# The even half of a real transform folded a second time: matmuls of 256 columns in place of 512, in a kernel whose order is planned

## The chip, the cores and the metric

The kernel runs on one core of a Trainium2 chip. A core has five engines that run side by side: PE (TensorE, matrix products into PSUM, with a weight load before each), DVE (VectorE), ACT (ScalarE), POOL (GpSimd) and SP (SyncE, which here only issues DMAs). The metric is the device time of one execution in microseconds (us).

## The reference

The input is one sequence `x` of 2048 rows (S) and 1024 columns (D), in bf16. Two branches are mixed by a gate:

```python
g = sigmoid((x * gate_w).sum(-1, keepdims=True))
a = irfft2(rfft2(x) * (w_r + 1j * w_i), s=(S, D))        # branch A: a 2-D spectral filter
Lam_bar = exp(dt * Lam);  B_bar = ((Lam_bar - 1) / Lam)[:, None] * Bmat
h[t] = Lam_bar * h[t - 1] + B_bar @ x[t]                 # branch B: a linear recurrence with 1024 complex states
b = 2 * (h @ Cmat.T).real + x * Dskip
out = g * a + (1 - g) * b
```

## The kernel before

**Branch B.** The states are cut into eight blocks `jb` of 128 and the sequence into four chunks `c` of 512. A turn `(jb, pr)` covers two chunks. `bu` computes `B x` for it on PE (L809: 16 matmuls of 512 columns for each chunk, real and imaginary), ACT copies the result from PSUM to a tile `u` (L812), and DVE turns it by a table of sines and cosines (`rot`, L777 to L783, through the scratch tile `su`, of which there is one), runs the recurrence as a real scan (L821) and passes the end state on as a carry. `rot_out` turns the states back. `table(jb)` makes the tables: nine ACT operations and three DVE operations for each block. There are three `u` tiles, so PE can run at most three turns ahead of DVE. At the end `yout(tb)` multiplies, for each of 16 row blocks, all states by C (L853, 32 matmuls of 512 columns), adds the skip term (L860), and DVE mixes in branch A (L880).

**Branch A.** The transform along D comes first. `halves(c)` writes, from the transposed input `xT`, the sums (L421) and differences (L423) of columns d and d + 512 into `xpm`: the sums give the even frequencies k, the differences the odd ones. `fd(j)`, for 16 strips j of 128 rows, multiplies each half by its matrix `G` (L560): four matmuls of 512 columns for each half (256 frequencies, real and imaginary), accumulated over four blocks of 128 columns. The rows of a strip are 16 apart in the sequence, so the weights of these matmuls are read from `xpm` at every 16th element. One ACT copy (L565) moves the strip to SBUF and interleaves even and odd frequencies. `s1(j)` does the first half of the transform along S (L575, L576: four matmuls of 512 columns), copied by ACT (L579; L580 saves one column) and written to DRAM. `s2w` reads back turned, finishes the transform (L700) and multiplies by the filter on DVE (L705); `is1`, `is2` and `idft` are the way back (L716, L735, L751, with ACT copies at L720, L739 and L756). Column 0 needs a repair, `fixup`, which uses `Wc`, two columns of the filter loaded in pieces of 2 bytes.

**The order.** Nothing of this is issued as it is written. Every helper records operations with an engine, a key, an assumed duration and the items it reads and writes. `Plan.run` then walks through time: it takes the engine on which something can start first, and of the operations that can start there (within a slack of 0.05 to 0.1 us on DVE and ACT) the one with the smallest key. The keys come from 28 numbers, `K_T0` to `K_GATE`, which place the stages against each other. So a changed duration or key moves the whole order on every engine, and SP's queue of DMAs with it. PSUM is four slots of two banks, shared by all stages.

Of the kernel before, what the change touches and what calls it, by code (L numbers as in the profile page):

```python
# [14 lines left out]
BF16 = mybir.dt.bfloat16  # L15
# [6 lines left out]
K = 512  # L22
NP = 1024
P = 128
TC = 512
# [10 lines left out]
def _host_consts():  # L36


    d = np.arange(K)[:, None]
    G = np.zeros((K, 2, 2, 256))  # L40
    for par in range(2):
        k = 2 * np.arange(256)[None, :] + par
        ang = 2 * np.pi * (((2 * d + 1) * k) % (2 * D)) / (2 * D)
        G[:, par, 0, :] = np.cos(ang)
        G[:, par, 1, :] = -np.sin(ang)
    G[:, 0, 1, 0] = (-1.0) ** np.arange(K)

    K4 = K // 2
    n = np.arange(K4)[None, :]
    Gi = np.zeros((2, 2, 2, P, K4))  # L50
    for par in range(2):
        for half in range(2):
            k = 2 * (np.arange(P)[:, None] + P * half) + par
            ang = 2 * np.pi * (((2 * n + 1) * k) % (2 * D)) / (2 * D)
            ck = np.where(k == 0, 1.0, 2.0)
            Gi[par, half, 0] = ck * np.cos(ang)
            Gi[par, half, 1] = -2.0 * np.sin(ang)
    Gi[0, 0, 1, 0, :] = (-1.0) ** np.arange(K4)
    Gi /= float(D * S)
    s1 = np.arange(P)[:, None, None, None]  # L60
    s2 = np.arange(16)[None, :, None, None]
    mh = 2 * np.arange(64)[None, None, None, :] + np.arange(2)[None, None, :, None]
    angF = 2 * np.pi * (((16 * s1 + s2) * mh) % S) / S
    TF = np.concatenate([np.sin(angF), np.cos(angF), -np.sin(angF)], axis=3)
    qq = np.arange(64)[:, None, None]
    bb = np.arange(32)[None, :, None]
    uu = np.arange(64).reshape(2, 2, 16).transpose(0, 2, 1).reshape(1, 1, 64)
    angI = 2 * np.pi * (((32 * qq + bb) * uu) % S) / S
    ci, si = np.cos(angI), np.sin(angI)
    MI = np.concatenate([np.concatenate([ci, -si, -ci], axis=2), np.concatenate([si, ci, -si], axis=2)], axis=0)  # L70
    p = np.arange(P)
    q = p // 8
    a = p % 8
    angK = 2 * np.pi * ((q[:, None] * q[None, :]) % 16) / 16
    delta = (a[:, None] == a[None, :]).astype(np.float64)
    Kc, Ks = delta * np.cos(angK), delta * np.sin(angK)
    ang16 = 2 * np.pi * (np.outer(np.arange(16), np.arange(16)) % 16) / 16
    RF = np.zeros((16, 2, 4, 2, 16, 4))
    for i in range(4):
        RF[:, 0, i, 0, :, i], RF[:, 1, i, 0, :, i] = np.cos(ang16), np.sin(ang16)  # L80
        RF[:, 0, i, 1, :, i], RF[:, 1, i, 1, :, i] = np.sin(ang16), -np.cos(ang16)
    ang32 = 2 * np.pi * (np.outer(np.arange(32), np.arange(32)) % 32) / 32
    RI = np.zeros((32, 2, 2, 2, 32, 2))
    for i in range(2):
        RI[:, 0, i, 0, :, i], RI[:, 1, i, 0, :, i] = np.cos(ang32), np.sin(ang32)
        RI[:, 0, i, 1, :, i], RI[:, 1, i, 1, :, i] = np.sin(ang32), -np.cos(ang32)
    sel = np.zeros((2, P, 2, 64))
    for odd in range(2):
        for c in range(2):
            sel[c, 2 * np.arange(64) + odd, odd, np.arange(64)] = 1.0 - 2.0 * c  # L90
    J = np.zeros((P, P))
    J[np.arange(P), 127 - np.arange(P)] = 1.0
    P0 = np.zeros((P, P))
    P0[(128 - np.arange(P)) % 128, np.arange(P)] = 1.0
    bf = lambda z: np.ascontiguousarray(np.ascontiguousarray(z, dtype=np.float32).astype(ml_dtypes.bfloat16))
    return dict(
        G=bf(G.reshape(4, P, 1024).transpose(1, 0, 2)),
        Gi=bf(Gi.reshape(8, P, K4).transpose(1, 0, 2)),
        TF=bf(TF),
        MI=bf(MI),  # L100
        TK=bf(np.stack([Kc, Ks, -Ks, J, P0, RF.reshape(P, P), RI.reshape(P, P)] + [z.reshape(P, P) for z in sel.reshape(2, P, P)], axis=1)),
    )
# [143 lines left out]
def kernel(  # L246
# [17 lines left out]
    nc = tc.nc  # L264
# [26 lines left out]
    def tile_of(shape, dtype, name, tag):  # L291
        group = plan.kinds[tag][0]
        if group == "m":
            return plan.buf(tag, lambda i: view(G_all[:, 1024 * (i - 4):1024 * (i - 3)], shape) if i >= 6 else
                            slots.tile(shape, dtype, name=name, tag=f"{group}{i}"))
        if group == "f":

            return plan.buf(tag, lambda i: view(hbuf[1].t[:, 2 + i // 4, i // 2 % 2, 1024 * (i % 2):1024 * (i % 2 + 1)], shape),
                            host=hbuf[1])
        return plan.buf(tag, lambda i: slots.tile(shape, dtype, name=name, tag=f"{group}{i}"))  # L300
# [11 lines left out]
    def pe(key, us, fn, r=(), w=()):  # L312
        plan.op("PE", key, us + 0.16, fn, r, w, gap=us)
# [4 lines left out]
    def dve(key, us, fn, r=(), w=()):  # L318
        plan.op("DVE", key, us, fn, r, w, gap=us - 0.085)
# [6 lines left out]

    U = 0.216
    A2 = nc.scalar.activation
    K_T0 = -49.82
    K_TB = 24.89  # L330
    K_D = 96.13
    K_O = 186.17
    K_TAB0 = 39.51
    K_TAB = -34.21
    K_F0 = 32.43
    K_F = 0.81
    K_W0 = 55.24
    K_W = 10.37
    K_WI = -61.0
    K_I0 = -398.94  # L340
    K_I = 45.74
    K_ID = 13.66
    K_CT = 34.07
    K_FIX = -104.41
    K_R1 = 397.68
    K_R2 = 838.32
    K_RS = 100.57
    K_Y = 840.08
    K_YS = 125.57
    K_H = 7.06  # L350
    K_XP = -10.85
    K_XS = -46.18
    K_TP = -92.54
    K_DM = 111.49
    K_BT = 77.09
    K_GATE = 165.55
    KX = lambda c: K_XP * (c > 0) + K_XS * max(c - 1, 0)


    vec8 = tile_of([8, 5, P], BF16, "vec8", "tt")  # L360
    for i, src in enumerate((B_Lambda_re, B_Lambda_im, B_log_dt, gate_w, B_Dskip)):
        dma(0, 0.05, lambda i=i, src=src: nc.scalar.dma_start(out=vec8.t[:, i, :], in_=src.rearrange("(j p) -> j p", p=P)),
            w=[(vec8, i)], eng="ACT", issue=0.33)
# [10 lines left out]
    G_sb = G_all.rearrange("p (d r k) -> p d r k", d=4, r=2)  # L374
# [41 lines left out]
    xT_of = lambda c: [("xT", c, q) for q in range(4)]  # L416
    xpm = tile_of([P, 2, 4, S], BF16, "xpm", "b32")

    def halves(c):
        lo, hi = xT[c][:, 0:4, :], xT[c][:, 4:8, :]  # L420
        dve(KX(c) + K_H, 1.22, lambda: nc.vector.tensor_add(out=xpm.t[:, 0, :, TC * c:TC * (c + 1)], in0=lo, in1=hi),  # L421
            r=xT_of(c), w=[(xpm, c, 0)])
        dve(KX(c) + K_H + 0.5, 1.22, lambda: nc.vector.tensor_sub(out=xpm.t[:, 1, :, TC * c:TC * (c + 1)], in0=lo, in1=hi),  # L423
            r=xT_of(c), w=[(xpm, c, 1)])

# [126 lines left out]
    mm = nc.tensor.matmul  # L552

    def fd(j, key):
        pf = psum([P, 2, 2, 256], "ps_fd")

        def f(par):
            xA = xpm.t.rearrange("p h d (a b) -> p h d b a", b=16)
            for db in range(4):
                mm(pf.t[:, par].rearrange("p c k -> p (c k)"), lhsT=xA[:, par, db, j, :],  # L560
                   rhs=G_sb[:, db, par, :], start=(db == 0), stop=(db == 3))
        for par in range(2):
            pe(key, 4 * U, lambda par=par: f(par), r=[(xpm, c, par) for c in range(4)] + [("G",)], w=[(pf, par)])
        X1 = tile_of([P, 2, K], BF16, "X1", "X1")
        act(key, 1.3, lambda: nc.scalar.copy(out=X1.t.rearrange("p c (k r) -> p r c k", r=2), in_=pf.t),  # L565
            r=[(pf, 0), (pf, 1)], w=[(X1,)])
        return X1
# [109 lines left out]
    for i in range(2):  # L677
        dma(30 + 16 * i, 3.0, lambda i=i: nc.sync.dma_start(out=MI_sb[i].t, in_=cst["MI"][:, 16 * i:16 * (i + 1)]),
            r=[("Bcol", 1)] if i else [], w=[(MI_sb[i],)])
# [205 lines left out]

    KB = lambda p, cc: K_T0 + K_TB * (p + 0.5 * cc)
    KD = lambda p: KB(p, 0) + K_D
    KF = lambda j: K_F0 + K_F * j
    KW = lambda b: K_W0 + K_W * b
    KI = lambda bp: K_I0 + K_I * bp  # L890
    halves(0)
# [8 lines left out]
    def turns_of(lo, hi):  # L900
        for p, (jb, pr) in list(enumerate(turns))[lo:hi]:
            if pr == 0:
                tabs[jb] = table(jb, K_TAB0 if jb == 0 else KB(p, 0) - K_TAB)
                if jb:
                    load_BT(jb, KB(max(p - 2, 0), 0) + K_BT)
            carries[jb] = bu(jb, pr, tabs[jb], carries.get(jb), (KB(p, 0), KB(p, 1)), KD(p))
            if pr == 0:
                rot_out(jb, 0, 1, KD(p) + K_O)
                rot_out(jb, 1, 1, K_R1 + K_RS * jb)
            else:  # L910
                rot_out(jb, 2, 2, K_R2 + K_RS * jb)

# [5 lines left out]
    for j in range(16):  # L918
        nxt = fd(j + 1, KF(j + 1)) if j + 1 < 16 else None
        s1(j, X1, KF(j + 1) + 1)  # L920
        X1 = nxt
    fixup(K_FIX)
    dma(130, 2.0, lambda: nc.sync.dma_start(out=G_all[:, 0:4 * K], in_=cst["Gi"].rearrange("p r k -> p (r k)")), r=[("Qz",)], w=[("G",)])
# [4 lines left out]
    for b in range(16):  # L928
        if b + 2 < 16:
            s2w(b + 2, KW(b + 2))  # L930
        is1(b, KW(b) + K_WI)
        if b % 2 and b + 3 < 16:
# [3 lines left out]
    for bp in range(16):  # L936
        nxt = is2(bp + 1, KI(bp + 1)) if bp + 1 < 16 else None
        idft(bp, ZT, KI(bp) + K_ID)
        if bp % 2 == 0:
            load_CT(bp // 2, KI(bp) + K_CT)  # L940
        ZT = nxt
    diag = make_diag(200)
    for tb in range(16):
        yout(tb, K_Y + K_YS * tb, diag)
    with tc.manual_schedule():
# [31 lines left out]
```

## Time and profile before

| what | value |
|---|---|
| median of 3 runs | 340.61 us (339.99 to 342.0) |
| the profiled execution | 340.25 us, span of its instructions 338.5 us |
| PE, matmuls | 327.6 us busy, 1917 instructions |
| PE, weight loads | 171.5 us |
| DVE | 292.0 us, 484 instructions |
| ACT | 192.7 us, 270 instructions |
| POOL | 17.0 us |
| granted TensorE clock | 1.00 |

The span runs from the first instruction to the last of the profiled execution. A matmul's duration in the profile goes on past the start of the next one, so durations of PE add up to more than the time they take; the distance from one start to the next is the step. A row of a group gives busy time, then the mean duration of one in ns, then the engine's idle time just before them and what ended it.

### The profile page before, as it was taken

The page shows a single profiled execution, that of the slowest core. Times are in us where ns is not written, and L with a number is a line of the kernel's source. Part 1 is how long each engine was busy: PE and PEld are TensorE (multiplying, and loading weights), DVE is VectorE, ACT ScalarE, POOL GpSimd, SP SyncE. Part 2 cuts the span into 40 slices and gives each one's busy share as a digit, 9 for nine tenths or more (in the row PEclk, how much of TensorE's full clock was granted, in tenths as well). Part 3 has the DMA queues.
Part 4 walks back from the last instruction along what each step waited for, and adds up shares of the span by engine and source line. Part 5 has one row for each costly group of instructions (what it writes and reads, how often), then busy time and mean ns, then how long its engine had stood idle before and what let it go on. Part 6 is the DMA issues. An engine that isn't in the chain of part 4 may idle for free.

```text
span 338.5 us, 5165 instructions
## 1 busy us (share of the span) xinstructions
PE 327.6 (97%) x1917; PEld 171.5 (51%) x1917; DVE 292.0 (86%) x484; ACT 192.7 (57%) x270; POOL 17.0 (5%) x36
## 2 busy tenths in 40 slices
PE   5999999999999999999998999999999999999994
PEld 4755465655444444444456576544544544445442
DVE  2899999997199999999999999999999999952321
ACT  3796999999887677999689999610000000000000
POOL 1157000000300000000000000000000000000000
PEclk9999999999999999999999999999999999999999
DMA  8995411993668999998487989961131024510001
GB/s 229 385 329 28 64 62 65 253 312 118 198 154 241 263 283 259 300 228 195 124 219 194 305 225 236 247 211 47 45 109 59 7 64 135 200 39 31 31 36 59
DMA packets 68705, 55.76 MB, mean 165 GB/s; under 512 B 46917, under 2 KB 51269, under 8 KB 68553
## 3 DMA queue, kind: packets, MB, share of 16 engines
q1 hardware_dynamic: 68600, 55.43, 60.1%
q8 instruction: 15, 0.25, 0.3%
q14 instruction: 10, 0.07, 0.1%
q10 hardware_dynamic: 80, 0.01, 0.0%
HBM read 30.77 MB, written 16.79 MB: 141 GB/s over the span
## 4 chain that ended last, share of the span: by engine, by line
PE 75%; ACT 13%; DVE 6%; issue 3%; DMA 1%; SPq 0%; DVEq 0%; ACTq 0%
PE ps_y L853 33%; PE psu L809 21%; PE ps_fd L560 7%; PE ps_id L751 3%; PE pt L403 2%; PE ps_y L860 2%; ACT A L579 2%; ACT u L812 1%; PE ps_is L716 1%; PE ps_s L575 1%; PE ps_s L576 1%; PE ps_is L735 1%; PE ps_is L717 1%; ACT ZT L739 1%; DVE h L821 1%
## 5 line engine op out<-in xcount | busy, mean ns | idle before, releaser
L809 PE MATMUL psu<-xT,BTs 128*128 128x512 bf16 x512 | 115.9, 379 | 0.6 <-ACT h L703 0.3
L853 PE MATMUL ps_y<-CT,h 128*128 128x512 bf16 x512 | 113.5, 379 | 0.0
L809 PEld LDWEIGHTS <-BTs 128*128 128x128 bf16 x512 | 49.6, 98 | 59.2 <-issue 1.6
L853 PEld LDWEIGHTS <-h 128*128 128x128 bf16 x512 | 49.2, 98 | 56.7 <-DVE h L779 0.5
L821 DVE TENSOR_TENSOR_SCAN h<-r_sb,carry,u 128x512 bf16<-128x512 f32 x48 | 59.5, 1270 | 0.0
L880 DVE SCALAR_TENSOR_TENSOR o<-ps_y,omg,ga 128x1024 bf16<-128x1024 f32 (+1 forms) x17 | 20.5, 1210 | 25.2 <-PE ps_y L860 25.2
L812 ACT CAST u<-psu 128x1024 bf16<-128x1024 f32 x32 | 32.5, 1019 | 11.0 <-PE psu L809 10.9
L560 PE MATMUL ps_fd<-G_all,xpm 128*128 128x512 bf16 x128 | 30.1, 379 | 0.0
L560 PEld LDWEIGHTS <-xpm 128*128 128x128 bf16 x128 | 18.4, 144 | 9.9
L777 DVE TENSOR_TENSOR su<-u,cs 128x2048 bf16<-128x2048 bf16 x16 | 19.4, 1215 | 2.8 <-ACT u L812 2.7
L565 ACT CAST X<-ps_fd 128x1024 bf16<-128x1024 f32 x16 | 21.3, 1340 | 0.2
L778 DVE TENSOR_TENSOR h<-h,pn 128x1024 bf16<-128x1024 bf16 (+1 forms) x24 | 20.6, 856 | 0.1
L777 DVE TENSOR_TENSOR su<-h,pn 128x1024 bf16<-128x1024 bf16 (+1 forms) x24 | 20.5, 856 | 0.1
L778 DVE TENSOR_TENSOR u<-u,cs 128x2048 bf16<-128x2048 bf16 x16 | 19.5, 1218 | 0.1
L821 DVE TENSOR_TENSOR_SCAN h<-r_sb,u 128x512 bf16<-128x512 f32 x16 | 19.0, 1210 | 0.0
L720 ACT CAST h<-ps_is 128x1024 bf16<-128x1024 f32 x16 | 15.8, 1014 | 2.3 <-PE ps_is L717 2.1
L579 ACT CAST A<-ps_s 128x1024 bf16<-128x1024 f32 x16 | 16.5, 1042 | 0.0
L703 ACT CAST h<-ps_s 128x1024 bf16<-128x1024 f32 x16 | 15.9, 1015 | 0.4 <-PE ps_s L700 0.3
L739 ACT CAST ZT<-ps_is 128x1024 bf16<-128x1024 f32 x13 | 12.9, 1046 | 2.6 <-PE ps_is L735 2.6
L751 PE MATMUL ps_id<-G_all,ZT 128*128 128x256 bf16 x104 | 12.8, 273 | 0.8 <-ACT ZT L739 0.8
L403 PE MATMUL pt<-ident,xn 128*128 128x128 bf16 x128 | 9.7, 243 | 3.7 <-DMA xn<-in_A_x_dram 3.5
L779 DVE TENSOR_TENSOR h<-h,su 128x512 bf16<-128x512 bf16 (+1 forms) x24 | 12.0, 501 | 0.2
(155 smaller groups left out, 388.0 us busy)
## 6 DMA issues: line engine op xcount, KB each, us to landing
xn<-in_A_x_dram SPq DMA_DIRECT2D x16, 256.0 KB, 4.6
turn_scratch<-A SPq DMA_DIRECT2D x16, 256.0 KB, 2.1
h<-turn_scratch SPq DMA_DIRECT2D x16, 256.0 KB, 5.6
turn_scratch<-h SPq DMA_DIRECT2D x16, 256.0 KB, 6.3
out_dram<-o SPq DMA_DIRECT2D x15, 256.0 KB, 2.1
eoc<-ga_scratch SPq DMA_DIRECT2D x12, 256.0 KB, 2.7
Cq<-turn_scratch SPq DMA_DIRECT2D x11, 256.0 KB, 3.6
ga_scratch<-eo SPq DMA_DIRECT2D x11, 256.0 KB, 2.7
```

The source lines that it names most:

```text
L403: nc.tensor.transpose(out=pt.t[:, j8, :], in_=src()[:, P * j8:P * (j8 + 1)], identity=ident)
L560: mm(pf.t[:, par].rearrange("p c k -> p (c k)"), lhsT=xA[:, par, db, j, :], rhs=G_sb[:, db, par, :], start=(db == 0), stop=(db == 3))
L565: act(key, 1.3, lambda: nc.scalar.copy(out=X1.t.rearrange("p c (k r) -> p r c k", r=2), in_=pf.t), r=[(pf, 0), (pf, 1)], w=[(X1,)])
L579: act(key, 1.01, lambda: nc.scalar.copy(out=A1.t, in_=psa.t), r=[(psa,)], w=[(A1,)])
L751: mm(pz.t[:, at, :], lhsT=ZT.t[:, 2 * par + half, c, :], rhs=Gi_sb[:, par, half, c, :], start=(half == 0), stop=(half == 1))
L777: dve(key, w, lambda: nc.vector.tensor_mul(out=sv(), in0=src()[:, ::-1], in1=bc(1)), r=sitem + [titem(1)], w=[(su,)])
L778: dve(key, w, lambda: nc.vector.tensor_mul(out=dst(), in0=src(), in1=bc(0)), r=sitem + [titem(0)], w=ditem)
L809: mm(psu.t[:, ri, :], lhsT=BT.t[:, ri, db, :], rhs=xT[c][:, db, :], start=(db == 0), stop=(db == 7))
L812: act(kb[cc], 1.01, lambda cc=cc, psu=psu: nc.scalar.copy(out=u.t[:, :, cc, :], in_=psu.t), r=[(psu, 0), (psu, 1)], w=ui(cc))
L821: dve(kd, 1.25, lambda cc=cc, ri=ri, carry=carry: nc.vector.tensor_tensor_scan(out=g()[:, ri, cc, :], data0=rb, data1=u.t[:, ri, cc, :], i ...
L853: mm(psy.t[:, 512 * dh:512 * (dh + 1)], lhsT=hbuf[jb // 4].t[:, jb % 4, ri, P * tb:P * (tb + 1)], rhs=CT[pc].t[:, ri, jb % 2, 512 * dh:512 ...
L880: dve(key - 1, 0.2 + 1.07e-3 * (b - a), lambda a=a, b=b: nc.vector.scalar_tensor_tensor(out=o.t[:, a:b], in0=psy.t[:, a:b], scalar=og, in1 ...
```

## The change

The even half is folded once more: of the sums, columns d and d + 256 are added and subtracted. The sums of these give k = 0, 4, 8, ..., the differences k = 2, 6, 10, ... . `halves` therefore writes the first sum into a new tile `both` (in the slot of `su`) and makes two further DVE operations of half its size from it. In `fd` the even half becomes two groups of two matmuls of 256 columns, where it was one group of four of 512; the odd half stays. So that the frequencies still lie in order, the output of each group goes to every second fp32 of the bank, and the columns of the even half of `G` are reordered. The assumed duration of the even half is halved, and all 28 numbers behind the keys are new.

```diff
+    G[:, 0] = G[:, 0].reshape(K, 2, 128, 2).transpose(0, 3, 1, 2).reshape(K, 2, 256)
...
-    K_D = 96.13
-    K_O = 186.17
+    K_D = -3.27
+    K_O = 228.08
...
     def halves(c):
         lo, hi = xT[c][:, 0:4, :], xT[c][:, 4:8, :]
-        dve(KX(c) + K_H, 1.22, lambda: nc.vector.tensor_add(out=xpm.t[:, 0, :, TC * c:TC * (c + 1)], in0=lo, in1=hi),
-            r=xT_of(c), w=[(xpm, c, 0)])
+        both = tile_of([P, 4, TC], BF16, "both", "su")
+        at = slice(TC * c, TC * (c + 1))
+        dve(KX(c) + K_H, 1.22, lambda: nc.vector.tensor_add(out=both.t, in0=lo, in1=hi), r=xT_of(c), w=[(both,)])
+        for g, fn in enumerate((nc.vector.tensor_add, nc.vector.tensor_sub)):
+            dve(KX(c) + K_H, 0.69, lambda g=g, fn=fn: fn(out=xpm.t[:, 0, 2 * g:2 * g + 2, at], in0=both.t[:, 0:2, :], in1=both.t[:, 2:4, :]),
+                r=[(both,)], w=[(xpm, c, 0, g)])
...
         def f(par):
             xA = xpm.t.rearrange("p h d (a b) -> p h d b a", b=16)
-            for db in range(4):
-                mm(pf.t[:, par].rearrange("p c k -> p (c k)"), lhsT=xA[:, par, db, j, :],
-                   rhs=G_sb[:, db, par, :], start=(db == 0), stop=(db == 3))
+            if par == 0:
+                for g in range(2):
+                    for db in range(2):
+                        mm(pf.t[:, 0].rearrange("p c (n g) -> p g c n", g=2)[:, g], lhsT=xA[:, 0, 2 * g + db, j, :],
+                           rhs=G_sb[:, db, 0, 256 * g:256 * (g + 1)], start=(db == 0), stop=(db == 1))
+            else:
+                for db in range(4):
+                    mm(pf.t[:, 1].rearrange("p c k -> p (c k)"), lhsT=xA[:, 1, db, j, :],
+                       rhs=G_sb[:, db, 1, :], start=(db == 0), stop=(db == 3))
         for par in range(2):
-            pe(key, 4 * U, lambda par=par: f(par), r=[(xpm, c, par) for c in range(4)] + [("G",)], w=[(pf, par)])
+            pe(key, (2 + 2 * par) * U, lambda par=par: f(par), r=[(xpm, c, par) + ((g,) if par == 0 else ()) for c in range(4) for g in range(2)] + [("G",)],
+               w=[(pf, par)])
```

More of the change, by code (lines that the diff above doesn't have):

```diff
@@ L328 @@
     A2 = nc.scalar.activation
-    K_T0 = -49.82
-    K_TB = 24.89
-    K_D = 96.13
-    K_O = 186.17
[L333 to L356, printed above, removed]
+    K_T0 = -30.23
+    K_TB = 25.57
+    K_D = -3.27
+    K_O = 228.08
+    K_TAB0 = 77.39
+    K_TAB = -27.68
+    K_F0 = 43.62
+    K_F = 1.51
+    K_W0 = -265.57
+    K_W = 24.23
+    K_WI = 29.65
+    K_I0 = -908.83
+    K_I = 56.75
+    K_ID = 55.0
+    K_CT = 127.78
+    K_FIX = -415.87
+    K_R1 = 658.93
+    K_R2 = 1222.58
+    K_RS = 22.26
+    K_Y = 642.04
+    K_YS = 96.38
+    K_H = 3.22
+    K_XP = -61.67
+    K_XS = -95.48
+    K_TP = -118.18
+    K_DM = 91.01
+    K_BT = 149.11
+    K_GATE = 236.6
     KX = lambda c: K_XP * (c > 0) + K_XS * max(c - 1, 0)
```

## The prediction, made before the changed kernel had run

> **What bounds the kernel now.** I read the page's engine totals first, then the chain of waits, then the groups by shape, and last the timelines of ACT and DVE through the stage that the change touches.
>
> ```profile
> PE 327.6 (97%) x1917; PEld 171.5 (51%) x1917; DVE 292.0 (86%) x484; ACT 192.7 (57%) x270; POOL 17.0 (5%) x36
> ```
>
> PE is filled, but a matmul's listed duration overlaps its successor, so I take its step from the chain:
>
> ```profile
> 41.37 2.59 PE ps_fd L560 x12
> 209.44 2.62 PE ps_id L751 x24
> ```
>
> That is 2.59/12 = 0.216 us for 512 columns and 2.62/24 = 0.109 for 256. The transposes and other 128-column matmuls step 0.056 in their timelines (8 in 0.45 us). All of PE is then 1312 x 0.216 + 128 x 0.109 + 400 x 0.056 + about 2.8 (gates and small ones) = 322.6 us. PE works from 3.6 to 334.2 us, so it waits only some 8 us in all: whatever shortens PE's own steps shortens the kernel, if ACT and DVE keep up. They have little room. First the groups by shape (busy us, mean ns of one):
>
> ```profile
> L560 PE MATMUL ps_fd<-G_all,xpm 128*128 128x512 bf16 x128 | 30.1, 379 | 0.0
> L560 PEld LDWEIGHTS <-xpm 128*128 128x128 bf16 x128 | 18.4, 144 | 9.9
> L735 PEld LDWEIGHTS <-Cq 128*128 128x128 bf16 x88 | 5.4, 98 | 1.9 <-issue 1.0
> L751 PE MATMUL ps_id<-G_all,ZT 128*128 128x256 bf16 x104 | 12.8, 273 | 0.8 <-ACT ZT L739 0.8
> L565 ACT CAST X<-ps_fd 128x1024 bf16<-128x1024 f32 x16 | 21.3, 1340 | 0.2
> L579 ACT CAST A<-ps_s 128x1024 bf16<-128x1024 f32 x16 | 16.5, 1042 | 0.0
> L421 DVE TENSOR_TENSOR xpm<-xT 128x2048 bf16<-128x2048 bf16 x4 | 4.9, 1218 | 0.0
> ```
>
> Then the timelines (start us, duration us, engine, line) of ACT in the loop of the forward transform and of DVE around it:
>
> ```profile
> 61.58 1.04 ACT L579 CAST A<-ps_s 128x1024 bf16<-128x1024 f32 x1
> 62.48 0.68 ACT L532 ACTIVATE tt<-tt 128x512 f32<-128x512 f32 x1
> 63.01 0.22 ACT L580 COPY Acol<-A 128x2 bf16<-128x2 bf16 x1
> 63.09 1.37 ACT L565 CAST X<-ps_fd 128x1024 bf16<-128x1024 f32 x1
> 64.26 1.06 ACT L579 CAST A<-ps_s 128x1024 bf16<-128x1024 f32 x1
> ...
> 23.31 1.22 DVE L423 TENSOR_TENSOR xpm<-xT 128x2048 bf16<-128x2048 bf16 x1
> 81.88 0.68 DVE L781 TENSOR_TENSOR h<-su,h 128x1024 bf16<-128x1024 bf16 x1
> 89.61 0.75 DVE L533 SCALAR_TENSOR_TENSOR tt<-tau_f,tht,tt 128x512 f32<-128x512 f32 x1 [7.05 <-ACT tt L532]
> 92.48 1.23 DVE L777 TENSOR_TENSOR su<-u,cs 128x2048 bf16<-128x2048 bf16 x1 [2.12 <-ACT u L812]
> ```
>
> From start to start a strip j costs ACT 1.17 (X) + 0.90 (A) + 0.08 (Acol) = 2.15 us, and one table operation of 0.53 between fills it to 2.6; PE needs (8 + 4) x 0.216 = 2.59. The two run level there. DVE is idle for 9 us just behind this stage, then solid until about 300.
>
> **The even half's matmuls.** In each of 16 strips four matmuls of 512 columns become four of 256: 64 in all. The columns streamed halve, but the output now goes to every second fp32 of the bank. No row of this trace writes PSUM at a step, so the step is bounded: 0.109 from below (L751, 256 adjacent columns) and 0.216 from above (L560, which crosses the same 512 places of a bank), a gain of 64 x 0.107 = 6.85 us or none. The stepped accesses that the trace does have point upwards: L560's weights, taken at every 16th element, load in 144 ns against 98 from adjacent places; L565's ACT copy, writing every second bf16, steps 1.17 against 0.90 of L579; only L735's weights, at every second bf16, cost nothing extra (98). Two of three pay 1.3 to 1.5 times, and of these the one that stays in no row of adjacent places pays most, so I take the upper end: 0 us gained. Both ends stay in the range.
>
> [...]
>
> The weight loads are the same 64 in number and stride. At a step of 0.216 their 144 ns are hidden; at 0.109 they might show, 0 to 64 x 0.035 = 2.2 us.
>
> **DVE.** Each of the four sums (L421, 1.14 start to start) is joined by a sum and a difference of 1024 elements (0.60 each by the L779 rows of that size): 4 x 1.2 = 4.8 us ahead of fd(0). The halves ended at 24.45; the new order fills about 0.9 us of waits that DVE had between 13 and 16 us, so they end near 24.45 + 4.8 - 0.9 = 28.35, while PE came to fd(0) at 28.26. The wait is 0.1 to 1.2 us; I take 0.2. Everything of DVE behind it slides by 3 to 4 us, into the idle 9 us at 82 to 92; without that idle it would be paid in full. The new tile shares the slot "su" with the rotations, but all its users are on DVE in order, so nothing waits.
>
> **The new order: ACT.** The stage order of the built kernel shows 23 table operations ahead of the end of s1(15), where there were 36: 13 of about 0.57 us, 7.3 us, leave the loop (ACT drops to 2.15 per strip) and go to 92-140 us, where ACT was busy 15 and 16 of each 20 us. Nine operations more (5.1 us) come after is2(0) than before. That stage ran from 174.97 to 219.9 = 44.9 us with 42.1 of ACT's steps and 41.9 of PE's, so 3 us of PE waits. In the new order ACT has 47.2 and PE 44.5 (more of the last turns and of ps_y's groups lie inside). With the same 2.9 on top of ACT it lasts 50.1, or 2.6 more wait than before; but part of ACT's surplus are diag operations and a table's tail that no matmul of the stage needs. Between 0 and 2.6 I take 0.8.
>
> **SP.** The four loads of Wc, which moved 2-byte pieces from 26.6 to 35 us, now stand ahead of the first two transposed loads of B. Those landed at 25.9 and 26.6, and so move by some 8.5 us to 34.4 and 35.1. Their reader bu10 moved too, behind fd(3): PE reaches it at 35.5 to 37. Hidden with a microsecond to spare; lost if Wc takes longer.
>
> **DVE's pacing of the end.** Before, the last rotation (7, c2-3) ended at 282.97 and PE's first group that reads it followed at about 282.9: no spare. Now DVE starts rotbu20 behind u's copy at about 92.2 (as before), has 199.1 us of queued steps to that rotation's end instead of 188.9, and 1.5 of gaps: 292.8. PE's order puts 282.1 us of steps ahead of the reader, plus 12.2 (the start at 3.6, the 7.6 us of waits of before, and the 1.0 of this sum) = 294.3. It holds by 1.5 us.
>
> **Sum.** 340.25 (profiled execution: 338.5 of span and 1.75 around it) + 0 (matmuls) + 0.2 + 0.8 = 341.25; the median of the runs lies 0.36 above that execution: 341.6 us. About 0.5%, 1.7 us, is what a measurement of this kernel tells from no change.
>
> **Rivals.** *A, the output step is free (0.109):* for it speak L751's row and that the columns streamed halve. PE falls to 315.8 us of steps, everything behind s1(15) comes 6 us sooner, ACT (2.15 per strip) just keeps level with PE (2.16), DVE starts rotbu20 near 86.1 and ends its last rotation at 286.7 against PE's 287.5. Time: 340.61 - 6.85 + 1.0 = 334.8, up to 337.0 if the 144 ns loads show. [...]
>
> *B, my forecast:* 341.6, own range 340.0 to 343.2.
>
> *C, slower, ACT becomes the bound from is2(0) to idft(15):* this decides once ACT's surplus over PE (2.7 us, 0.2 before) is not taken up by operations that nobody awaits. With the matmuls at 0.216 the price is 2.6 us or, if the eo copies queue behind whole tables as well, up to PE's full 5: 343.4 to 346. Against it: ps_y groups stand between the last idft steps.
>
> *D, a step between the ends:* at the 1.3 to 1.5 times of the stepped rows, 0.142 to 0.160, the gain is 3.6 to 4.7, giving 337 to 338.
>
> **How the numbers follow.** A 0.30, D 0.08, B 0.42, C 0.20. A gives 0.28 to faster and 0.02 to same; D 0.06 and 0.02; B 0.02, 0.24 and 0.16 to slower; C all to slower. Together 0.36 faster, 0.28 same, 0.36 slower. The range runs from A's 333.5, with all of its terms a little better, to 345 within C. It leaves out the ends of A and C, less than 2 in 10.
>
> **What the new profile would show.** The step of even-half matmuls, start to start, settles A against B: 0.109 or 0.216 (anything clearly between is D). The first ps_fd should start at 28.3 to 29.5, behind the DVE difference. ACT in the strips should be full at 2.15 only if A holds, and show idle time before X and A if B holds. The span from the first is2 to the last idft should be 45 to 47 us; 49 or more is C. I am wrong in the mechanism if bu10 waits for a DMA, or if ps_y groups of blocks 8 to 10 wait for DVE's rotations by more than a microsecond.

## The result, and the profile after

The changed kernel takes **342.05 us** (median of 20 runs, 340.88 to 344.96) against 340.46 us for the kernel before (20 runs): the ratio is 1.0049, with a 95% interval of 1.0031 to 1.0067. It is slower by 1.6 us, and the 64 matmuls of half as many columns brought nothing back. The profiled execution has a span of 340.0 us (338.5 before) at a granted clock of 1.00.

The page of the changed kernel, engine totals:

```profile
PE 327.7 (96%) x1917; PEld 172.9 (51%) x1917; DVE 297.8 (88%) x492; ACT 192.3 (57%) x270; POOL 23.7 (7%) x36
```

PE's busy time is what it was. DVE has eight instructions and 5.8 us more, POOL 6.7 us more for the same 36. The chain of waits of the changed kernel has the first strip in it (start, duration, what):

```profile
28.46 0.86 PE ps_fd L567 x4
29.32 0.86 PE ps_fd L571 x4
```

L567 are the four matmuls of 256 columns, L571 the four of 512. Both groups take 0.86 us, so the step is 0.216 us either way. It is not a lower clock: the granted clock is 1.00, and the 512 columns beside them step 0.216 as before. The groups by shape say the same (busy us, mean ns of one, idle before):

```profile
L567 PE MATMUL ps_fd<-G_all,xpm 128*128 128x256 bf16 x64 | 16.5, 411 | 0.0
L571 PE MATMUL ps_fd<-G_all,xpm 128*128 128x512 bf16 x64 | 17.1, 389 | 0.0
L577 ACT CAST X<-ps_fd 128x1024 bf16<-128x1024 f32 x16 | 21.0, 1323 | 2.0 <-PE ps_fd L571 2.0
L591 ACT CAST A<-ps_s 128x1024 bf16<-128x1024 f32 x16 | 16.2, 1015 | 2.7 <-PE ps_s L588 2.6
L426 DVE TENSOR_TENSOR xpm<-both 128x1024 bf16<-128x1024 bf16 x8 | 5.3, 689 | 0.0
```

A matmul of 256 columns is listed at 411 ns, above the 389 of one with 512 and far above the 273 that 256 adjacent columns took before. ACT's copies X and A, which had waited 0.2 and 0.0 us, now wait 2.0 and 2.7 us for PE. In the timeline of ACT this looks like so (the bracket is idle time before the instruction and what ended it):

```profile
56.17 1.32 ACT L577 CAST X<-ps_fd 128x1024 bf16<-128x1024 f32 x1
57.34 0.20 ACT L592 COPY Acol<-A 128x2 bf16<-128x2 bf16 x1
57.85 1.01 ACT L591 CAST A<-ps_s 128x1024 bf16<-128x1024 f32 x1 [0.31 <-PE ps_s L588]
58.76 1.32 ACT L577 CAST X<-ps_fd 128x1024 bf16<-128x1024 f32 x1
```

A strip still comes every 2.59 us (56.17 to 58.76), now set by PE alone: the table operation that stood between the copies has gone, and nothing took its place.

Where the 1.6 us come in is found by taking PE start to start and subtracting, for each matmul, the median step of its kind (the gate's 32 small matmuls, which take 1.86 us before and 1.83 after, are left out). What is left are PE's waits, by stage (us):

| stage | before | after |
|---|---|---|
| up to the first ps_fd (28.3) | 2.69 | 2.79 |
| the strips, to 92 | -0.05 | 0.00 |
| 92 to 140 | 1.03 | 1.93 |
| 140 to the first is2 | 0.95 | 0.95 |
| first is2 to last idft | 3.12 | 3.81 |
| the end | -0.02 | -0.10 |

The sum is 7.72 before and 9.38 after: 1.66 us more, and the whole difference of the two kernels. It lies in two places, 0.90 us between 92 and 140 and 0.69 us in the stage of is2 and idft. PE's timeline of the changed kernel shows four of these waits:

```profile
106.58 0.60 PE L712 MATMUL ps_s<-h,TK_sb 128*128 128x512 bf16 x2 [0.21 <-DMA h<-turn_scratch]
113.91 3.61 PE L821 MATMUL psu<-xT,BTs 128*128 128x512 bf16 x16 [0.24 <-ACT u L824]
119.84 0.38 PE L821 MATMUL psu<-xT,BTs 128*128 128x512 bf16 x1 [0.59 <-ACT h L732]
175.90 0.29 PE L747 MATMUL ps_is<-TK_sb,Cq 128*128 128x128 bf16 x2 [0.81 <-DMA Cq<-turn_scratch]
```

Two wait for ACT, two for a DMA. ACT is indeed full there: windows from 100 to 125 us, before and then after (window, then length and busy time of PE, PEld, DVE, ACT, POOL, the clock, DMA share and GB/s):

```profile
100.00:125.00 25.00, 24.56 (x132) 11.17 (x130) 25.00 (x44) 18.77 (x30) 0.00 (x0) 1.00 0.95 260
```

```profile
100.00:125.00 25.00, 23.75 (x126) 10.43 (x124) 24.58 (x45) 24.12 (x40) 0.00 (x0) 1.00 0.97 265
```

ACT has ten instructions and 5.35 us more in these 25 us, for the most part table operations that left the strips.

### The profile page after: what moved, and what is told of

It is laid out like the page before. It is cut to its first block, busy times and chain, and to the rows that moved or that the text cites. A ratio compares the mean times of both kernels' runs of the same rounds, so it can differ in the third digit from the quotient of the medians.

```text
span 340.0 us, 5180 instructions
## 1 busy us (share of the span) xinstructions
PE 327.7 (96%) x1917; PEld 172.9 (51%) x1917; DVE 297.8 (88%) x492; ACT 192.3 (57%) x270; POOL 23.7 (7%) x36
## 4 chain that ended last, share of the span: by engine, by line
PE 63%; ACT 11%; DMA 10%; DVE 9%; issue 4%; SPq 2%; ACTq 0%; DVEq 0%
PE ps_y L865 33%; PE psu L821 10%; PE ps_fd L567 4%; PE ps_fd L571 4%; DMA wB<-in_A_w_i_dram 4%; PE ps_id L763 3%; DVE h L833 2%; DMA wA<-in_A_w_r_dram 2%; PE ps_y L872 2%; PE ps_s L588 2%; PE ps_s L587 2%; ACT ZT L751 2%; PE pt L404 2%; ACT u L824 2%; DMA Cq<-turn_scratch 1%
## 5 line engine op out<-in xcount | busy, mean ns | idle before, releaser
L833 DVE TENSOR_TENSOR_SCAN h<-r_sb,carry,u 128x512 bf16<-128x512 f32 x48 | 59.8, 1271 | 0.0
L577 ACT CAST X<-ps_fd 128x1024 bf16<-128x1024 f32 x16 | 21.0, 1323 | 2.0 <-PE ps_fd L571 2.0
L833 DVE TENSOR_TENSOR_SCAN h<-r_sb,u 128x512 bf16<-128x512 f32 x16 | 18.8, 1209 | 0.0
L591 ACT CAST A<-ps_s 128x1024 bf16<-128x1024 f32 x16 | 16.2, 1015 | 2.7 <-PE ps_s L588 2.6
L571 PE MATMUL ps_fd<-G_all,xpm 128*128 128x512 bf16 x64 | 17.1, 389 | 0.0
L567 PE MATMUL ps_fd<-G_all,xpm 128*128 128x256 bf16 x64 | 16.5, 411 | 0.0
L751 ACT CAST ZT<-ps_is 128x1024 bf16<-128x1024 f32 x13 | 14.1, 1115 | 0.0
L768 ACT ACTIVATE eo<-ps_id,gA 128x1024 bf16<-128x1024 f32 x11 | 13.0, 1219 | 0.0
```

The costliest lines, as they stand in the source:

```text
L567: mm(pf.t[:, 0].rearrange("p c (n g) -> p g c n", g=2)[:, g], lhsT=xA[:, 0, 2 * g + db, j, :], rhs=G_sb[:, db, 0, 256 * g:256 * (g + 1)], ...
L571: mm(pf.t[:, 1].rearrange("p c k -> p (c k)"), lhsT=xA[:, 1, db, j, :], rhs=G_sb[:, db, 1, :], start=(db == 0), stop=(db == 3))
L751: act(key, 1.01, lambda: nc.scalar.copy(out=ZT.t.rearrange("p kc c (q g) -> p kc (c q) g", g=2), in_=psz.t.rearrange("p kc g q -> p kc q g ...
L833: dve(kd, 1.25, lambda cc=cc, ri=ri, carry=carry: nc.vector.tensor_tensor_scan(out=g()[:, ri, cc, :], data0=rb, data1=u.t[:, ri, cc, :], i ...
```

## Experiments

Three questions were open. Does the stepped output really set the step of 0.216, and what is it worth without the step? Is the loss of 1.6 us the fold's work on DVE, or ACT's table operations in their new place? And how much is the order's own doing? The theory at the outset: the stepped output alone undoes the gain, DVE's extra work is swallowed, and ACT's moved operations make the loss. The rival: the step of 0.216 has another cause (the strided weight loads), and the loss is DVE's.

**Adjacent output columns.** From the changed kernel, with its order: the matmuls write adjacent columns (the columns of both halves of `G` are reordered alike), and ACT's copy puts the frequencies in order instead.

```diff
-                        mm(pf.t[:, 0].rearrange("p c (n g) -> p g c n", g=2)[:, g], ...
+                        mm(pf.t[:, 0, g, :], ...
-    nc.scalar.copy(out=X1.t.rearrange("p c (k r) -> p r c k", r=2), in_=pf.t)
+    nc.scalar.copy(out=X1.t.rearrange("p c (n g r) -> p r g c n", g=2, r=2), in_=pf.t.rearrange("p r g (c n) -> p r g c n", c=2))
```

> The changed kernel with the same order, but both halves of fd write adjacent places of PSUM (the columns of G of both halves are reordered alike) and the ACT copy that leaves PSUM puts every frequency in its place. If the step of the PSUM output is what made the 256-column matmuls take 0.216 us (theory T1), their step falls to 0.109, the fd stage shortens by up to 6.8 us and the time falls to 334 to 337 us; the loop is then level between PE (2.16 us a strip) and ACT (2.15, more if the copy's wider step in SBUF costs). If it is the weight loads at every 16th element (rival T2), the weights being the same, the step stays 0.14 to 0.216 and the time 339 to 342.

Measured: 349.5 us, 1.0273 times before (1.0235 to 1.0312), outside both forecasts. Two rows of its groups:

```profile
L568 PE MATMUL ps_fd<-G_all,xpm 128*128 128x256 bf16 x64 | 9.6, 272 | 0.7 <-ACT Acol L593 0.7
L578 ACT CAST X<-ps_fd 128x1024 bf16<-128x1024 f32 x16 | 39.5, 2500 | 0.0
```

The same matmuls with the same strided weights now step 0.109 us: the stepped output was the whole cause, and the weight loads of 144 ns do not show even at that rate. But the copy X, which now writes every fourth bf16, went from 1323 to 2500 ns and made ACT the bound: a strip took 3.22 us.

**The same, with the copy written end to end.** One line more: both sides of the copy run through the strip in the order of the output.

```diff
-    nc.scalar.copy(out=X1.t.rearrange("p c (n g r) -> p r g c n", g=2, r=2), in_=pf.t.rearrange("p r g (c n) -> p r g c n", c=2))
+    nc.scalar.copy(out=X1.t.rearrange("p c (n g r) -> p c n g r", g=2, r=2), in_=pf.t.rearrange("p r g (c n) -> p c n g r", c=2))
```

> As the run with adjacent outputs, where the matmuls stepped 0.109 but the ACT copy, which then wrote every fourth bf16, took 2.50 us instead of 1.32 and became the loop's bound. Here the copy goes through the same places in another order: it writes X1 from end to end and picks its reads from four runs of PSUM. If the copy's price hangs on the step of what it writes, it falls to some 1.04 us (as L579 and the other copies that write from end to end), ACT needs 1.9 a strip against PE's 2.16, and the time falls to 333.5 to 337. If reading PSUM out of order costs as much, the copy stays at 2 to 2.5 and the time at 346 to 350.

Measured: **335.9 us, 0.9868 times before (0.9833 to 0.9903)**, the best of all versions. Its groups, and a line of PE's timeline:

```profile
L568 PE MATMUL ps_fd<-G_all,xpm 128*128 128x256 bf16 x64 | 9.7, 273 | 0.0
L578 ACT CAST X<-ps_fd 128x1024 bf16<-128x1024 f32 x16 | 16.0, 1015 | 0.7 <-PE ps_fd L572 0.2
```

```profile
35.03 0.38 PE L588 MATMUL ps_s<-X,TF_sb 128*128 128x512 bf16 x1 [2.38 <-ACT X L578]
```

The copy costs 1015 ns, as much as one with nothing to reorder (A, 1017 ns), and a strip takes 2.16 us. The gain on paper is 6.85 us from 342.05; 6.15 came. The wait of 2.4 us at the first strips is new: X stood on ACT behind a table operation that waited 2.95 us for POOL's `ci`. POOL was late by one operation:

```profile
20.80 6.48 POOL L481 TENSOR_TENSOR lbi<-r_sb,sn 128x8 f32<-128x8 f32 x1 [5.79 <-ACT sn L473]
```

In the changed kernel, with the same order on every engine, it took 0.73 us. So the wait belongs to this execution (337.15 us, in runs from 334.32 to 338.66) and not to the order; why the operation took so long is not shown.

**The copy's order alone.** The kernel before, with only that reordering of the copy.

```diff
-    nc.scalar.copy(out=X1.t.rearrange("p c (k r) -> p r c k", r=2), in_=pf.t)
+    nc.scalar.copy(out=X1.t.rearrange("p c (k r) -> p c k r", r=2), in_=pf.t.rearrange("p r c k -> p c k r"))
```

> The kernel before, no fold, keys and order as before; only its ACT copy of fd goes through the same places in the other order: it writes X1 from end to end and reads the two halves of PSUM by turns. If the step of the writes is what makes it 1.34 us, it falls to 1.04 and takes 16 x 0.3 = 4.8 us off ACT in a stage where ACT and PE are level: 338.5 to 340.5. If reading by turns costs, 341 or more.

Measured: 340.53 us, 1.0002 (0.9984 to 1.002).

```profile
L565 ACT CAST X<-ps_fd 128x1024 bf16<-128x1024 f32 x16 | 16.1, 1009 | 1.6 <-PE ps_fd L560 1.3
```

331 ns less in each of 16 copies, 5.3 us of ACT, are worth nothing while PE's step is 0.216. So in the version with adjacent columns it is the matmuls that gain, and the copy only keeps ACT from taking it back.

**How fine the step may be.** The kernel before, its `idft`: one half of the matmuls writes every second fp32 of a bank, the other half writes pairs of fp32, two places on and two off.

```diff
-                    mm(pz.t[:, at, :], ...
+                    mm(to, ...       # par 0: "p (n g) -> p g n", par 1: "p (n g q) -> p g n q" with q=2
```

> The kernel before, with only the outputs of the idft matmuls (256 columns, weights from adjacent places, step 0.109) moved: for the even half to every second fp32 of one bank, for the odd half to pairs of neighbours with a gap of two between pairs in the other bank. The columns of branch A come out in another order than the reference's. T1: the 64 of the even half step 0.216, the time grows by some 7 us (64 x 0.107) to 347; the 64 in pairs tell the grain: 0.109 if two neighbours are enough, 0.216 if any gap costs (then 354). T2 expects 0.109 for all and 340.5.

Measured: 345.05 us in one run, 4.6 more than the 340.45 of the kernel before measured beside it and less than the 7 forecast. The stage of is2 and idft grew from 44.9 to 50.0 us; with 6.85 us more of PE's steps in it, its waits fell from 3.12 to about 1.4. PE's timeline has eight matmuls of 256 columns, four of each kind:

```profile
178.92 1.46 PE L752 MATMUL ps_id<-G_all 128*128 128x256 bf16 x8
180.22 1.06 PE L735 MATMUL ps_is<-TK_sb,Cq 128*128 128x128 bf16 x16
```

From 178.92 to 180.22 are 1.30 us = 4 x 0.216 + 4 x 0.109; start to start, the first kind steps 0.216 and the pairs 0.109. So not every gap costs: two places on and two off step 0.109 us, as adjacent columns do in the kernel before, and one on and one off 0.216, twice that. No other grain was tried.

**DVE's extra work, four ways.** First as planned operations in the kernel before, with the old keys, so that the order was planned anew:

> The kernel before with the fold's extra DVE work alone: the first sum is written once to the scratch tile and then again in two halves to xpm, 4.8 us more of DVE ahead of fd(0); PE, ACT and the keys as before (the planner may move a few operations). If the idle 9 us of DVE at 82 to 92 swallow it, 340.6 to 341.2; if DVE's pacing of the end is felt, up to 345.

Measured: 343.57 us, 1.008 (1.0062 to 1.0097). The order had moved as well, so the price of the work could not be read from it. Then the changed kernel without the fold's two DVE operations (the even half is left unfolded), also planned anew:

> The changed kernel without the fold's arithmetic: the even half gets one sum on DVE as before (4.8 us less of DVE), the matmuls are those of the change, so the even half's values are wrong. If the fold's DVE work is the cost also in the new order, it comes back to 339 to 340.5; if the new order has swallowed it and the table operations of ACT moved late are the cost, it stays at 341.5 to 342.5.

Measured: 345.18 us, 1.0143 (1.013 to 1.0156). Taking work away made it slower by 3 us, which neither forecast had. Both are lessons about the planner and not about DVE. So the next two hold the order of every engine fixed. The kernel before with the work added inside one planned operation:

```diff
-        dve(KX(c) + K_H, 1.22, lambda: nc.vector.tensor_add(out=xpm.t[:, 0, :, ...], in0=lo, in1=hi), ...
+        def f():
+            nc.vector.tensor_add(out=xpm.t[:, 0, :, at], in0=lo, in1=hi)
+            for g in range(2):
+                nc.vector.tensor_add(out=xpm.t[:, 0, 2 * g:2 * g + 2, at], in0=lo[:, 2 * g:2 * g + 2, :], in1=hi[:, 2 * g:2 * g + 2, :])
+        dve(KX(c) + K_H, 1.22, f, ...
```

> The kernel before, its order of work kept instruction by instruction: each of the four first sums of the first transform is followed, within the same planned step, by two sums over half as many columns (the sizes that the folded version has), so that VectorE has some 4.8 us more to do ahead of the first fd matmul and nothing else differs. Theory 1 (VectorE's surplus is swallowed by its idle 9 us at 82 to 92): 340.5 to 341.0, the first fd matmul up to 0.3 us later. Theory 2 (VectorE's pacing of the strips and of the end passes the surplus on): 342 to 343.6, with the end later by 1.5 us or more.

Measured: 343.64 us, 1.0094 (1.0076 to 1.0113). In that order the work is not swallowed: PE waits 2.56 us in the strips, where it had waited none. The way it takes is in the timelines of this kernel:

```profile
35.63 0.74 DVE L550 SCALAR_TENSOR_TENSOR pn<-tf,ncr,tt 128x512 bf16<-128x512 f32 x1
36.40 0.72 ACT L535 ACTIVATE tt<-tau_f,tht 128x512 f32<-128x512 f32 x1 [4.04 <-DVE pn L550]
...
46.82 1.46 PE L565 MATMUL ps_fd<-G_all,xpm 128*128 128x512 bf16 x6 [1.54 <-ACT u L817]
```

The tail of a table (`pn`) stands on DVE behind the scan; later DVE makes it later (35.63, where the kernel before had it at 31.77). ACT's first operation of the next table waits for it 4.04 us instead of 0.64, with every copy behind it in ACT's queue, and PE at last waits for the copies. DVE's slack at 82 to 92 comes too late to help: the stall is passed on inside the strips. The counterpart is the changed kernel, order kept, with the fold's two operations cut to 16 columns (the even half is left unfolded):

```diff
-        ... nc.vector.tensor_add(out=both.t, in0=lo, in1=hi)
+        ... nc.vector.tensor_add(out=xpm.t[:, 0, :, at], in0=lo, in1=hi)
-        ... fn(out=xpm.t[:, 0, 2 * g:2 * g + 2, at], in0=both.t[:, 0:2, :], in1=both.t[:, 2:4, :])
+        ... fn(out=xpm.t[:, 0, 2 * g:2 * g + 2, TC * c:TC * c + 16], in0=lo[:, 0:2, 0:16], in1=lo[:, 2:4, 0:16])
```

> The changed kernel, its order kept: the first sum goes straight to the matmuls' tile and the two folded ops are cut to 16 columns, so that VectorE has some 4.3 us less to do ahead of the first fd matmul. The even half of the transform is left unfolded, so its numbers are not the reference's. Theory 1 (the fold's VectorE work is swallowed): 341.5 to 342. Theory 2 (it is the loss against before): 339 to 340.5, with y beginning 1 us or more earlier than in the changed kernel.

Measured: 341.89 us, 1.0048 (1.0033 to 1.0064), the changed kernel's own 1.0049. There 4.2 us of DVE work cost nothing. In the changed kernel `pn` stands ahead of the scan (L550 at 31.45, the scan L833 at 33.32), and the next table's first operation comes at 38.58 and waits for nothing, so the chain of the last fence does not exist. Where the work had been hidden shows in DVE's timeline once it is gone:

```profile
30.57 0.75 DVE L547 SCALAR_TENSOR_TENSOR pn<-tf,cr,tt 128x512 bf16<-128x512 f32 x1 [2.35 <-ACT tt L545]
92.82 1.23 DVE L789 TENSOR_TENSOR su<-u,cs 128x2048 bf16<-128x2048 bf16 x1 [2.65 <-ACT u L824]
```

With the fold's work the first of these starts at 30.79 and waits for nothing: DVE did the work in time that it would else spend waiting for ACT's table. The second waits 2.65 us in both; DVE's idle time from 82 to 92.8, 3.66 us, is the same with the work and without it.

**ACT's surplus.** The changed kernel, order kept: seven of ACT's nine operations of the tables of blocks 3 to 7 work on half of the columns, and the ops behind them read the half twice, so these tables are not the reference's.

```diff
+        w = TC if jb < 3 else TC // 2
-        act(key, 0.72, lambda: A2(out=kk(), in_=tau_f, func=ACT.Identity, ...
+        act(key, 0.72, lambda: A2(out=kh(), in_=tau_f[:, 0:w], func=ACT.Identity, ...
...
```

> The changed kernel, its order kept: of the tables of blocks 3 and up, seven of ScalarE's nine ops work on half of the columns, and the ops after them read the half twice, which takes some 0.25 us from each, about 7 us from ScalarE in the stretches 100 to 125 and 174 to 222. These tables are not the reference's. Theory 1 (ScalarE's surplus in those stretches is the later start of y, 1.6 us): 340.2 to 341, the stage from is2(0) to idft(15) back from 48.2 to about 47. Theory 2 (the surplus is hidden; the order of PE's steps and the DMA of Cq make the later start): 341.7 to 342.2.

Measured: 341.29 us, 1.0021 (1.0 to 1.0043). A window and a wait of it:

```profile
100.00:125.00 25.00, 23.93 (x127) 10.56 (x126) 24.18 (x44) 22.27 (x40) 0.00 (x0) 1.00 0.95 261
```

```profile
120.45 0.81 PE L825 MATMUL psu<-xT,BTs 128*128 128x512 bf16 x3 [0.60 <-ACT h L736]
```

The time lies between the two expectations, and its interval touches both that of the changed kernel and 1. By stages, 92 to 140 still waits 1.74 us (1.93) although ACT has 1.85 us less in the window, and the largest wait there, 0.59 us for the copy `h`, is the same 0.60. What ACT won it lost again 2 us ahead of that copy, in an idle 1.12 us for DVE's product `wA` (L721): in this order the shorter operations do not bring the copy sooner. The stage from 140 to the first is2 rises from 0.95 to 1.33, and that of is2 and idft falls from 3.81 to 2.90 us. But the latter also falls to 3.12 in the experiment before, which does nothing to ACT in that stage; there the wait for the DMA of `Cq` was only 0.32 us where it had been 0.97. So the medians put some 0.8 (342.05 - 341.29) of the 1.6 us on the length of ACT's operations, and even that is not settled.

**The keys.** The changed kernel with the 28 numbers of before, and the kernel before with the new ones:

> The changed kernel with the 28 numbers of the kernel before. If the surplus of 1.6 us over the kernel before comes from the new keys' order (table operations of ACT moved late), this one is nearer to the kernel before: 340 to 341.5. If the fold's own work is the cost, or the old keys suit the fold worse, 342 or more.

> The kernel before with the 28 numbers of the changed one. The fold's work alone cost 3.1 us in the old order and the change with the old keys 3.5, with the new ones 1.6. If the new keys are better by themselves, this one gains what they gave there, some 2 us: 338 to 339.5. If they only suit the folded kernel, it is slower than the kernel before: 341 to 346.

Measured: 343.97 us, 1.0112 (1.0085 to 1.0138), and 367.12 us, 1.0787 (1.0773 to 1.0801). The new numbers save the folded kernel 1.9 us and cost the unfolded one 26.8. They fit one kernel and say nothing of another. The second time lies far outside both forecasts, and not all of it is waiting: its four runs have a mean granted clock of 0.967. In its trace PE waits 4.45 us for ACT up to 124.01; from 124 to 147 the granted clock is 0.57, and matmuls of 512 columns step 0.43 us there.

**The best version, its cost told to the planner.** The copy's assumed 1.30 us set to the 1.01 that it takes, so that the order is planned anew:

```diff
-        act(key, 1.3, lambda: nc.scalar.copy(out=X1.t.rearrange("p c (n g r) -> p c n g r", g=2, r=2), ...
+        act(key, 1.01, lambda: nc.scalar.copy(out=X1.t.rearrange("p c (n g r) -> p c n g r", g=2, r=2), ...
```

> The version with adjacent PSUM columns and the X copy that writes end to end, the planner's cost of that copy lowered from 1.30 to 1.01, which is what it took, so that the order of work is planned anew for it. If the order of before loses by the wrong cost (the stall of 2.5 us at 32 would be the first to go): 333 to 335.5. If an order planned with a truer cost is as likely worse as better, as with the two changes of keys: 335 to 340.

Measured: 341.17 us, 1.0008 (0.9987 to 1.0029), outside both forecasts: a truer number lost 5.3 us. The strips kept their gain (the last s1 at 79.2 us, against 85.5 in the changed kernel; the 81.5 of the version above has the late `lbi` in it, which took 0.73 us here), and the next stages spent it. A line of PE's timeline:

```profile
212.74 1.68 PE L764 MATMUL ps_id<-G_all 128*128 128x256 bf16 x7 [2.63 <-ACT G_all L752]
```

In the new order ACT has skip-term tiles and copies `u` and `eo` ahead of the copies that the last idft steps need, and PE waits 9.7 us in the stage of is2 and idft, where the changed kernel has 3.81. Behind the wait of the fence PE is slow as well: from 212.5 to 216 the granted clock is 0.56, 256 columns step 0.213 us and 128 step 0.107, which takes 1.4 us more than their usual 0.109 and 0.056. Nine of the 12 runs have a mean granted clock of 0.993 to 0.995 and take 340.70 to 342.09 us, the other three, at 0.999 and 1.000, 339.27 to 340.21. So about 1.4 of the 5.3 us are the clock.

## Why the prediction was right, and where it was not

**The even half's matmuls: right.** The forecast of 341.6 us stood on this one choice, 0.216 of the two ends and nothing gained; 342.05 came. The prediction took the upper end by analogy with stepped weight loads and ACT's stepped writes. Those pay 1.3 to 1.5 times (144 ns against 98 for the loads, 1.17 us against 0.90 for the writes), which alone spoke for a step between the ends (rival D); that it is twice was a choice that came out, and no row of before could show it. The run with adjacent columns shows that the output's step is the cause, and the one with pairs shows how fine it may be. Rival A was priced at 334.8 us and up to 337.0 for a free step; the version in which the step is 0.109 takes 335.9, but with a cheaper copy than A had; with ACT as the bound the same step gave 349.5.

**Weight loads: right.** They load in 155 ns and stay hidden at 0.216, and in 144 ns at 0.109 as well.

**DVE ahead of fd(0): right in size.** The first ps_fd starts at 28.29 us (28.35 was forecast for the halves; 28.26 before), so the wait is 0.04 where 0.2 was taken. **The cover was named wrongly.** It was to be DVE's idle 9 us at 82 to 92, "without that idle it would be paid in full". With that idle almost whole (8.7 us of 9.2) 3.3 us (343.64 - 340.38, the kernel before measured beside it) are paid in the order of before. In the changed order it is not the cover either, since it stays at 3.66 us with the work and without it. What takes most of the work up there is DVE's wait for ACT's table at 30.6 us, early in the strips (2.35 us without the work, none with it). That `pn` stands ahead of the scan, and that no table of ACT waits for it there, keeps the work from being passed on; which of these two does more was not tried apart.

**ACT: the sum nearly right, its places not.** For the stage of is2 and idft 0.8 us of new waits were taken, and 0.69 came, though mostly as the wait for `Cq`, which is a DMA, and not for ACT; that the size agrees is luck. The stage lasts 48.2 us, outside the 45 to 47 that was to confirm it: those bounds left out that PE's own steps in the stage grow from 41.9 to 44.5, which the same paragraph had counted. 44.9 + 2.6 + 0.8 is 48.3. The step that failed is the other one: the thirteen table operations that move to 92 to 140 were given no price, because ACT had been busy only 15 and 16 of 20 us there. They filled it (24.1 of 25 us), and 0.90 us of new waits lie in that stretch. The relieved version takes back 0.19 of them. That the rest is owed to where these operations stand and what they wait for is the likely reading, but not shown: no run puts them back into the strips with the rest of the order held. Rival C, ACT as the bound, did not come about.

**SP: right.** The four loads of B were issued from 28.24 to 36.0 us, behind `Wc`, and PE's turn at 36.93 followed the strip with no wait.

**DVE's pacing of the end: held, with less to spare.** The last rotation ended at 294.70 us (292.8 was worked out). By the prediction's own sum with the waits that came, 3.5 + 282.1 + 9.4, PE reaches its reader at some 295.0, an estimate, so 0.3 us is left of the 1.5; PE's ps_y row of the changed kernel has 0.0 us of idle time before it.

**The sum.** 1.0 us was taken on top of before and 1.6 came. The missing 0.6 is the unpriced 0.90 between 92 and 140, less 0.16 for DVE's smaller wait and 0.11 in the stage of is2 and idft. The forecast of the time came 0.15 nearer than that of the change, because it started from 340.61, the median of three runs, where twenty give 340.46.

## What to carry to other kernels

A matmul's price follows where its output goes as well as its columns: here 256 columns stepped 0.109 us into adjacent places or pairs, and into every second fp32 0.216, as 512 do. Before halving the columns, see that the halves land in adjacent places or at least in pairs of fp32, and let the copy out of PSUM do the reordering by reading out of order and writing in order (1.01 us here, against 1.32 written at every second element and 2.50 at every fourth). Work added to an engine "with slack" is free only if nothing queued behind it is awaited before the slack is reached (here some 5 us more of DVE work cost 3.3 us in one order, and 4.2 us nothing in another); follow the queue from the added operation to the first one that another engine waits for. And where a planner sets the order, an experiment that changes a planned cost or operation measures the new order first; keep the order fixed to price anything smaller than the several microseconds that orders differ by.

## What the hardware showed that was not expected

- Output of 256 fp32 columns to PSUM: 0.109 us a step if adjacent, 0.109 in pairs with gaps of two between them, 0.216 at every second fp32.
- ACT's copy of 128x1024 from PSUM to bf16 in SBUF: 1.01 us written end to end (1.04 in the version with its cost told), 1.32 to 1.34 at every second element, 2.50 at every fourth. The order in which PSUM was read made no difference (1.009 and 1.015 us by turns from two and from four places, 1.015 straight).
- The granted clock, 1.00 in most of these traces, fell to 0.57 behind a PE wait of 4.45 us (the new keys alone) and to 0.56 behind one of 2.63 us (the cost told): 512 columns then step 0.43 us, 256 step 0.213 and 128 step 0.107. Behind the wait of 2.38 us at 35 (the copy written end to end) it did not fall: 512 columns went on at 0.216.
- The first 28 us vary from one execution to the next: PE's waits there were 2.79 us in the changed kernel and 3.67 in the version with ACT relieved, whose work and order are the same up to that point.
- One small POOL operation (`lbi`) is listed at 6.48 us in one execution and at 0.73 in another of the same order, and PE waited 2.4 us behind it.
